# Pooled attention and two gated MLPs on one core: the order of work on every engine written out, piece by piece

## The chip, the cores and the metric

One Trainium2 chip, one of its cores. The metric is the device time of one execution, in microseconds (us). The kernel before takes 1108.62 us, the median of three runs (1107.89 to 1112.15). All weights and activations are computed on the core; nothing is prepared on the host except that float64 weights are passed as raw words.

## The reference, cut to what matters

```python
# q, k, v: [8 batches, 8 heads, 576, 64]
k_p = k.reshape(B, H, 72, 8, D).mean(axis=3)          # pooled keys and values
v_p = v.reshape(B, H, 72, 8, D).mean(axis=3)
scores = q @ k_p.T / sqrt(D)
attn = exp(scores - max(scores)); attn /= sum(attn) + 1e-9
x = concat_heads(attn @ v_p)                          # [8, 576, 512]
# first MLP
h = relu(x @ w_in)                                    # [8, 576, 1024]
conv = sum_k conv_w[k] * h[:, s + k - 1, :]           # 3 taps along the sequence, zero padded
x = (h * sigmoid(conv)) @ w_out                       # [8, 576, 512]
# second MLP
h = gelu_tanh(x @ w_in2)                              # [8, 576, 1024] -> u | v, 512 each
v = (v - mean(v)) / sqrt(var(v) + 1e-6) * g_ln
v = einsum('ts,bsd->btd', w_sg, v) + b_sg[:, None]    # along the sequence
out = x + (u * v) @ w_out2
```

## The kernel before, in words

Precision. Nearly every product is made of three TensorE matmuls on a high and a low part (`mm3`, L99 to L103, and the triples that `mm_sum`, L105 to L108, and `mm_halves`, L110 to L118, get). The high part is a ScalarE copy to the 32-bit matmul type, the low part a subtraction on VectorE or GpSimd (`subtract`, L141; `split`, L144). Weights come as float64 words and are put together on VectorE by three bit operations (`to_f32`, L172, L174, L176), then split.

Phase 1 is attention and the first MLP. Attention goes by batch, 8 batches: keys and values are pooled on GpSimd (`k_pool`, `v_pool`, L261 to L265), transposed on TensorE into `KBT` (`k_fin`, L285 to L288); queries are transposed in 32x32 blocks on VectorE (L340); then for each of five row tiles scores (`s_mm`, L361), maximum (L365), exponential (L376, or L370 with the sum accumulated in ScalarE), normalisation on GpSimd (`s_norm`, L387, L390), TensorE transposes (`e_tr`, L403, L409) and, for four head pairs, the product with the values (`a_mm`, L108 with tile `psa`, L435, L436). Its result goes into `xT`, which holds two batches. The MLP goes by 12 chunks of 384 rows, so three chunks are two batches; each chunk has eight slices f of the hidden width: `i_mm(c, f)` (L108 with tile `psi`, then L458, L468 on ScalarE, L469, L470 on VectorE, L471 on ScalarE, L474 on VectorE, a ScalarE copy and a GpSimd subtraction into `hg`) and `o_mm(c, f)` (L101 to L103 with tile `pso`). PSUM holds two banks for attention (tag `a`), three for `i_mm` (tag `i`) and three for `o_mm`.

Phase 2 is the second MLP by batch: `v_mm`, `u_mm`, `sp_mm`, `o2_mm`, on PSUM tiles `ps` of two banks. Its inputs are read back from DRAM (`x2s`), transposed on VectorE (`x2_fetch`, `x2_split`, L688) and split. Between the phases the spatial weights `w_sg` are transposed on TensorE (`sg_step`, L637, L640).

What sets the order. The function calls are written in program order (`phase1`, `att_steps`), but the tile framework is opened with a scheduler that runs a timeline model at build time and orders the instructions of each engine itself, one by one:

```python
with _tile.TileContext(nc, schedule_with_timeline_sim=True) as tc:
    pooled_attention_gated_mlps(tc, *args)
```

So in the trace matmuls of three `i_mm` calls and one `a_mm` call alternate singly. On the chip each engine then works through its own list in that order, and an instruction whose inputs are not there holds what stands behind it. All loads and stores are issued from SP's queue, in order too; pooled inputs go through two buffers (tag `raw`).

Of the kernel before, what the change touches and what calls it, by code (L numbers as in the profile page):

```python
# [38 lines left out]
):  # L39

# [27 lines left out]
    XW = 2 * (S + 2)  # L68

# [12 lines left out]
    def bank(tag, bufs):  # L82
        return psum1.tile([128, 512], F32, tag=tag, bufs=bufs, name=f"ps{tag}")

    def a_bank():
        return bank("a", 2)

    def i_bank():
        return bank("i", 3)
# [31 lines left out]

    ident = const.tile([128, 128], F32, name="ident")
# [20 lines left out]
    def split(hi, lo, x, eng=nc.vector):
        nc.scalar.copy(out=hi, in_=x)  # L144
        subtract(lo, x, hi, eng)


    def setup():
        nc.gpsimd.memset(mhalf, -0.5)
        nc.scalar.activation(out=warm, in_=mhalf, func=AF.Exp)  # L150
        make_identity(nc, ident)
        nc.vector.tensor_reduce(
            out=mask,
            in_=ident[0:96, 0:96].rearrange("p (k h j) -> p h k j", k=3, h=4),
            axis=AX.XY,
            op=ALU.add,
        )
        nc.gpsimd.memset(KBT, 0.0)
        for t in (Vh, Vl):
            nc.gpsimd.memset(t.bitcast(F32), 0.0)  # L160
# [17 lines left out]

    early = {}

    def load_coef():
        n = 3 * NF
        early["c"] = work.tile([128, 1, 512], F32, tag="y", name="cf")
        raw = early["cr"] = att2.tile([128, 1024], U32, tag="raw", name="craw")
        nc.sync.dma_start(out=raw[0:n, 0:256], in_=conv_w.rearrange("k (m p) -> (k m) p", p=256))
        nc.sync.dma_start(out=early["c"][n:n + NU, 0, 0:128], in_=g_ln.rearrange("(m p) -> m p", p=128))

    def setup_coef():
        n = 3 * NF
# [23 lines left out]
    def conv_weight(key, pool, tag, eng=None, bank_=None):  # L213
        raw = raws.pop(key)
        t = work.tile([128, 512], F32, tag="y", name="t")
        to_f32(raw, t, bank_)
        hl = pool.tile([128, 2, 512], F32R, tag=tag, name=f"{tag}hl")
        split(hl[:, 0, :], hl[:, 1, :], t, eng or nc.vector)
        return hl
# [15 lines left out]

    def load_pool(src, b, i, raw=None):


        if raw is None:
            raw = att2.tile([128, 2, 512], F32, tag="raw", name="raw")  # L240
# [15 lines left out]
        return raw  # L256

    def pool_sum(eng, raw, dst, n):
# [4 lines left out]
        eng.tensor_tensor(out=a[:, :, 0:256], in0=a[:, :, 0:256], in1=a[:, :, 256:512], op=ALU.add)  # L263
        eng.tensor_tensor(out=a[:, :, 0:128], in0=a[:, :, 0:128], in1=a[:, :, 128:256], op=ALU.add)
        eng.tensor_tensor(out=dst, in0=a[:, :, 0:64], in1=a[:, :, 64:128], op=ALU.add)  # L265
# [3 lines left out]
    def k_pool(b, i, eng, raw=None):  # L269
# [3 lines left out]
        if raw is None:  # L273
            raw = load_pool(k, b, i)
        if i < 2:
            pool_sum(eng, raw, kv["kp"][:, 2 * i:2 * i + 2, :], 128)
        else:
            pool_sum(eng, raw, kv["kr"], 32)

    def k_fin(b):  # L280
# [5 lines left out]
        nc.tensor.transpose(kt[:, :, 64:SP], kr.rearrange("p a d -> p (a d)"), ident[0:32, 0:32])  # L286
        nc.scalar.copy(out=KBT[0:64, :, 0:SP], in_=kt[0:64])
        nc.vector.tensor_copy(out=KBT[64:128, :, SP:2 * SP], in_=kt[64:128])  # L288

    def v_pool(b, i, eng, raw=None):  # L290
        if i == 0:
            kv["vp"] = att1.tile([128, NP_, D], F32, tag="vp", name="vp")
        if raw is None:
            raw = load_pool(v, b, i)
        if i < 2:
            pool_sum(eng, raw, kv["vp"][:, 2 * i:2 * i + 2, :], 128)
        else:
            kv["vr"] = att1.tile([96, 2, D], F32, tag="kr", name="vr")
            pool_sum(eng, raw, kv["vr"], 96)

    def v_fin(b, eng):
        vp = kv["vp"]
        for par in range(2):
            P = slice(64 * par, 64 * par + 64)
            split(Vh[P, :, 64 * par:64 * par + 64], Vl[P, :, 64 * par:64 * par + 64], vp[P])
        vrm = work.tile([96, NP_, 128], F32, tag="y", name="vrm")
        eng.tensor_tensor(
# [4 lines left out]
        )  # L312
        nc.scalar.copy(out=VR, in_=vrm)
        subtract(VR[32:64], vrm[32:64], VR[32:64])
# [5 lines left out]
    def q_load(b):  # L320
# [21 lines left out]

    def q_load0(t):
        t0, n = TT[t]
        nc.sync.dma_start(out=early["q"][0:n, t, :].rearrange("p (h d) -> p h d", h=H),
                          in_=q[0, :, t0:t0 + n, :].rearrange("h s d -> s h d"))

    es = {}

    def s_mm(b, t, act):  # L350


        n = TT[t][1]
        qT = qTs.pop((b, t))
        e = att2.tile([128, H, SP], F32, tag="e", name="e")
        sm = stat.tile([128, H], F32, tag="sm", name="sm")
        for a in range(2):
            ps = a_bank()
            for x in range(2):
                p = 2 * a + x  # L360
                nc.tensor.matmul(out=ps[0:n, 2 * SP * x:2 * SP * x + 2 * SP], lhsT=qT[:, p, 0:n], rhs=KBT[:, p, :],  # L361
                                 start=True, stop=True)
            sv = ps[0:n, 0:4 * SP].rearrange("p (x j) -> p x j", j=SP)
            mx = stat.tile([128, 4], F32, tag=f"mx{a}", name="mx")
            nc.vector.tensor_reduce(out=mx[0:n], in_=sv, axis=AX.X, op=ALU.max)  # L365
            if act:
                nc.vector.tensor_scalar(out=mx[0:n], in0=mx[0:n], scalar1=-EXP_SCALE, scalar2=None, op0=ALU.mult)
                for x in range(4):
# [3 lines left out]
            else:  # L372
                nc.vector.tensor_tensor(out=e[0:n, 4 * a:4 * a + 4, :], in0=sv, in1=bc(mx[0:n], 2, SP),  # L373
                                        op=ALU.subtract)
        if not act:
            nc.scalar.activation(out=e[0:n], in_=e[0:n], func=AF.Exp, scale=EXP_SCALE)  # L376
            nc.vector.tensor_reduce(out=sm[0:n], in_=e[0:n], axis=AX.X, op=ALU.add)
        es[b, t] = (e, sm)

    def s_norm(b, t, eng):  # L380
        n = TT[t][1]
        e, sm = es[b, t]
        rs = stat.tile([128, H], F32, tag="rs", name="rs")
        nc.vector.tensor_scalar(out=sm[0:n], in0=sm[0:n], scalar1=1e-9, scalar2=None, op0=ALU.add)
        nc.vector.reciprocal(out=rs[0:n], in_=sm[0:n])
        en = att2.tile([128, 512 + 192], F32, tag="en", name="en")
        eng.tensor_tensor(out=en[0:n, 0:512].rearrange("p (h j) -> p h j", h=H), in0=e[0:n, :, 0:64],  # L387
                          in1=bc(rs[0:n], 2, 64), op=ALU.mult)
        for c in range(2):
            eng.tensor_tensor(  # L390
# [5 lines left out]
    def e_tr(b, t):  # L396
# [5 lines left out]
        for c in range(NP_):  # L402
            nc.tensor.transpose(ps[:, 128 * c:128 * c + n], en[0:n, 128 * c:128 * c + 128], idn)  # L403
        m = ps.rearrange("p (c s) -> p c s", c=NP_)[:, :, 0:n]
        nc.scalar.copy(out=eTh[:, 0:NP_, T], in_=m)
        subtract(eTl[:, :, T], m, eTh[:, 0:NP_, T])
        ps = a_bank()
        for c in range(2):
            nc.tensor.transpose(ps[0:96, 128 * c:128 * c + n], en[0:n, 512 + 96 * c:608 + 96 * c], idn)  # L409
# [498 lines left out]
```

## Time and profile before

| | |
|---|---|
| median of three runs | 1108.62 us |
| the profiled execution's own time | 1111.01 us |
| its span, first to last instruction | 1109.2 us |
| TensorE busy | 996.8 us (90%) |
| VectorE busy | 670.4 us (60%) |
| ScalarE busy | 431.7 us (39%) |
| GpSimd busy | 316.5 us (29%) |
| mean granted TensorE clock | 0.957 of full speed |
| moved by DMA | 86.65 MB, mean 78 GB/s |

The profile is one execution. "Busy" of TensorE counts a matmul from its start to its modelled end, and neighbours overlap, so what a matmul costs in a dense stretch is read from the distance of starts, not from its duration. The granted clock has two levels, 1.00 (2.4 GHz) and 0.50 (1.2 GHz); a mean between them says for how much of a stretch the lower one held.

### The profile page before, as it was taken

The numbers are of one execution on the slowest core, as the hardware profiler recorded it, in microseconds if no ns is written. First come the engines' busy times: TensorE is split into PE (matmuls) and PEld (weight loads), VectorE is DVE, ScalarE is ACT, GpSimd is POOL, SyncE is SP. The second block draws the span as 40 slices with busy tenths as digits, with TensorE's granted clock in tenths as the row PEclk, the third lists the DMA queues.
The fourth block names the chain that finished last, engine by engine and source line by source line (L and its number), as shares of the span: only waits on it lengthen the run. The fifth ranks groups of instructions, "written<-read, shape, count | busy, mean of one in ns | idle before, by whom it ended". The sixth has DMA issues, their size and how long they took to land.

```text
span 1109.2 us, 14835 instructions
## 1 busy us (share of the span) xinstructions
PE 996.8 (90%) x5446; PEld 890.8 (80%) x5446; DVE 670.4 (60%) x1258; ACT 431.7 (39%) x892; POOL 316.5 (29%) x418
## 2 busy tenths in 40 slices
PE   3467789999799988999897996999999999999997
PEld 2356679889689877898887885989898989999896
DVE  4949967648387376684665946764634545373523
ACT  2444446535266354555554643422222222231210
POOL 3357646426267155462240320100100010000000
PEclk9998989999689999899998997999999999999999
DMA  9944227014133134130004039241414231322021
GB/s 220 259 113 90 54 63 104 29 53 99 45 65 74 48 71 105 44 77 29 29 29 158 6 76 233 33 102 33 110 29 111 42 108 32 87 33 95 1 76 57
DMA packets 182836, 86.65 MB, mean 78 GB/s; under 512 B 150800, under 2 KB 154924, under 8 KB 182764
## 3 DMA queue, kind: packets, MB, share of 16 engines
q1 hardware_dynamic: 182764, 85.71, 30.9%
q8 instruction: 43, 0.70, 0.3%
q14 instruction: 29, 0.24, 0.1%
HBM read 66.81 MB, written 18.87 MB: 77 GB/s over the span
## 4 chain that ended last, share of the span: by engine, by line
PE 71%; DVE 9%; DMA 6%; SPq 5%; POOL 3%; ACT 3%; issue 2%; DVEq 0%; POOLq 0%; ACTq 0%
PE ps L114 20%; PE psi L108 13%; PE ps L101 6%; PE ps L103 6%; PE ps L102 6%; PE pso L103 4%; PE pso L102 4%; PE pso L101 4%; PE psa L108 3%; DMA raw<-in_k_dram 2%; SPq L324 2%; PE psa L361 2%; DMA raw<-in_v_dram 2%; DVE psi L470 1%; POOL raw L263 1%
## 5 line engine op out<-in xcount | busy, mean ns | idle before, releaser
L141 POOL TENSOR_TENSOR hg<-g,hg 128x384 fp32r<-128x384 f32 x96 | 99.9, 1042 | 112.7 <-ACT hg L144 112.6
L759 POOL TENSOR_SCALAR rstd<-mv 128x2 f32<-128x2 f32 (+1 forms) x20 | 8.0, 398 | 371.4 <-DVE mv L757 371.4
L800 DVE SCALAR_TENSOR_TENSOR y<-ps,coef,bsg 128x576 f32<-128x576 f32 x32 | 26.2, 818 | 125.6 <-PE ps L114 125.6
L114 PE MATMUL ps<-w2sh,v 128*128 128x288 f32 x512 | 94.5, 296 | 0.0
L361 PE MATMUL psa<-KBT,qT 128*128 128x144 f32 (+1 forms) x320 | 60.9, 332 | 28.3 <-DVE e L373 17.7
L361 PEld LDWEIGHTS psa<-KBT,qT 128*128 128x128 f32 (+1 forms) x320 | 51.8, 209 | 36.7 <-issue 20.7
L114 PEld LDWEIGHTS ps<-w2sh,v 128*128 128x128 f32 x512 | 76.9, 189 | 0.0
L263 POOL TENSOR_TENSOR raw<-raw 128x512 f32<-128x512 f32 (+2 forms) x42 | 53.8, 1288 | 75.4 <-DMA raw<-in_v_dram 41.0
L436 DVE SCALAR_TENSOR_TENSOR xl<-psa,xh 128x288 fp32r<-128x288 f32 x64 | 29.3, 458 | 75.8 <-ACT xh L435 74.9
L469 DVE SCALAR_TENSOR_TENSOR psi<-h,coef,psi 128x384 f32<-128x384 f32 x96 | 58.7, 612 | 18.6 <-ACT psi L468 18.0
L144 ACT CAST hg<-g 128x384 fp32r<-128x384 f32 x96 | 49.1, 512 | 48.4 <-DVE g L474 47.5
L787 ACT ACTIVATE u<-ps 128x576 f32<-128x576 f32 x32 | 20.9, 652 | 115.9 <-PE ps L114 115.9
L471 ACT ACTIVATE psi<-psi 128x384 f32<-128x384 f32 x96 | 45.3, 472 | 52.0 <-DVE psi L470 51.8
L470 DVE SCALAR_TENSOR_TENSOR psi<-h,coef,psi 128x384 f32<-128x384 f32 x96 | 58.7, 614 | 1.0
L474 DVE SCALAR_TENSOR_TENSOR g<-psi,h 128x384 f32<-128x384 f32 x96 | 52.4, 546 | 10.0 <-ACT psi L471 9.3
L458 ACT ACTIVATE h<-psi 128x386 f32<-128x386 f32 (+1 forms) x96 | 46.3, 491 | 27.3 <-PE psi L108 27.2
L468 ACT ACTIVATE psi<-h,coef 128x384 f32<-128x384 f32 x96 | 55.6, 583 | 2.0
L144 ACT CAST gt<-y 128x576 fp32r<-128x576 f32 (+2 forms) x48 | 23.1, 512 | 85.1 <-DVE y L802 85.1
L114 PE MATMUL ps<-w2sl,v 128*128 128x288 f32 x256 | 54.9, 295 | 0.0
L435 ACT ACTIVATE xh<-psa 128x288 fp32r<-128x288 f32 x64 | 26.4, 412 | 72.4 <-PE psa L108 70.9
L387 POOL TENSOR_TENSOR en<-e,rs 128x512 f32<-128x512 f32 (+1 forms) x40 | 42.5, 1064 | 38.8 <-PE psa L409 16.2
L365 DVE TENSOR_REDUCE mx<-psa 128x4 f32<-128x288 f32 (+1 forms) x80 | 35.6, 450 | 25.3 <-PE psa L361 24.6
(414 smaller groups left out, 3011.0 us busy)
## 6 DMA issues: line engine op xcount, KB each, us to landing
xb<-x2s SPq DMA_DIRECT2D x128, 72.0 KB
x2s<-ob SPq DMA_DIRECT2D x32, 256.0 KB
res<-x2s SPq DMA_DIRECT2D x16, 512.0 KB
out_dram<-ob SPq DMA_DIRECT2D x16, 512.0 KB
qb<-in_q_dram SPq DMA_DIRECT2D x112, 72.0 KB
raw<-in_k_dram SPq DMA_DIRECT2D x28, 256.0 KB
raw<-in_v_dram SPq DMA_DIRECT2D x28, 256.0 KB
raw<-in_v_dram SPq DMA_DIRECT2D x48, 64.0 KB
```

The source lines that it names most:

```text
L101: nc.tensor.matmul(out=out_, lhsT=ah, rhs=bh, start=first, stop=False)
L102: nc.tensor.matmul(out=out_, lhsT=al, rhs=bh, start=False, stop=False)
L103: nc.tensor.matmul(out=out_, lhsT=ah, rhs=bl, start=False, stop=last)
L108: nc.tensor.matmul(out=out_, lhsT=a, rhs=b_, start=(i == 0), stop=(i == n - 1))
L114: nc.tensor.matmul(out=ps[:, hf, 0:HS], lhsT=a, rhs=b_[:, hf * HS:(hf + 1) * HS], start=(i == 0), stop=(i == n - 1),)
L141: eng.tensor_tensor(out=out, in0=in0, in1=hi.bitcast(F32), op=ALU.subtract)
L144: nc.scalar.copy(out=hi, in_=x)
L263: eng.tensor_tensor(out=a[:, :, 0:256], in0=a[:, :, 0:256], in1=a[:, :, 256:512], op=ALU.add)
L361: nc.tensor.matmul(out=ps[0:n, 2 * SP * x:2 * SP * x + 2 * SP], lhsT=qT[:, p, 0:n], rhs=KBT[:, p, :], start=True, stop=True)
L468: nc.scalar.activation(out=y, in_=tap(1), func=AF.Copy, scale=cw(1, f))
L469: nc.vector.scalar_tensor_tensor(out=y, in0=tap(0), scalar=cw(0, f), in1=y, op0=ALU.mult, op1=ALU.add)
L470: nc.vector.scalar_tensor_tensor(out=y, in0=tap(2), scalar=cw(2, f), in1=y, op0=ALU.mult, op1=ALU.add)
```

## The change: what it does

Every function becomes a generator (a *task*) that yields wherever the work passes from one engine to another; the stretch between two yields is a *piece*, and all of its instructions are on one engine. A string `ORDER` names tasks by letter, slice and batch or chunk (`I6.4` is slice 6 of `i_mm` in chunk 4; `s0.5` is score tile 0 of batch 5); each time a name comes up, its next piece is issued. `step` adds to each instruction an ordering edge without a semaphore to the one before it on the same engine, so the scheduler can no longer move it. SP's queue is ordered the same way.

Beside that:

- PSUM: attention has three banks, `i_mm` two (before two and three).
- The low parts of all 16 weight slices of the first MLP are subtracted on GpSimd (before: 8 on VectorE, 8 on GpSimd), and `to_f32` keeps its intermediate in the output tile in SBUF (before: in a PSUM bank of tag `i`).
- Score tiles 0, 2 and 4 of batch 1 too take the exponential with the sum accumulated on ScalarE (before: those of batch 0 alone).
- Of the keys of batch b+1 one half is loaded and pooled ahead of the score tiles of batch b, the rest between and behind the last of them; the values of batch b are pooled ahead of its score tiles.
- `w_sg` is loaded into buffers of tag `ob` and transposed among the pieces of chunks 10 and 11 (before: in the steps around and behind the last `o_mm` calls).
- Phase 2 has the same calls in the same TensorE order.

```diff
+ORDER = '''z k0.0 k1.0 k2.0 p0.0 c z z p1.0 v0.0 p2.0 v1.0 p3.0 v2.0 p4.0 i0 i1 z z i2 ... i7 q.1 t0 ... t7 k0.0
...
+ e0.5 I4.5 e0.5 O5.4 O5.4 p3.5 e0.5 I4.5 s1.5 e0.5 s2.5 s1.5 I4.5 I5.5 s2.5 I4.5 I4.5 s2.5 I5.5 e1.5 s2.5 O6.4
+ O6.4 I4.5 I5.5 s2.5 I4.5 e1.5 s2.5 I6.5 I5.5 I5.5 s2.5 e1.5 I5.5 p4.5 e1.5 s3.5 I6.5 q.6 O7.4 I5.5 s3.5 e1.5
...
+ o0.7 o1.7 o0.7 m2.7 m2.7 o0.7 o2.7 o1.7 o1.7 o2.7 o2.7'''
...
+    ACT_SUM = {(0,0),(0,2),(0,4),(1,0),(1,2),(1,4)}
...
     def a_bank():
-        return bank("a", 2)
+        return psum1.tile([128, 512], F32, tag="a", bufs=3, name="psa")
     def i_bank():
-        return bank("i", 3)
+        return psum1.tile([128, 512], F32, tag="i", bufs=2, name="psi")
...
+    LO_IN = [pool for f in range(NF)]
+    LO_OUT = [pool for f in range(NF)]
...
+    def weight(pool_, tag, src, eng, bank_, done):
+        raw = pool_.tile([128, 1024], U32, tag=tag, name=f"{tag}raw")
...
+        nc.sync.dma_start(out=dst, in_=src)
+        yield
         t = work.tile([128, 512], F32, tag="y", name="t")
-        to_f32(raw, t, bank_)
...
+        yield from to_f32(raw, t, bank_() if bank_ else None)
+        hl = pool_.tile([128, 2, 512], F32R, tag=tag, name=f"{tag}hl")
+        done(hl)
+        nc.scalar.copy(out=hl[:, 0, :], in_=t)
+        yield
+        subtract(hl[:, 1, :], t, hl[:, 0, :], eng)
...
+    def t_w_in(f, *_):
...
+        return weight(in1, f"wi{f}", src, LO_IN[f], None, done)
...
-    def i_mm(c, f):
+    def t_i(f, c):
...
         mm_sum(ps[:, 0:w], prs)
+        yield
...
         nc.scalar.activation(out=y, in_=tap(1), func=AF.Copy, scale=cw(1, f))
+        yield
         nc.vector.scalar_tensor_tensor(out=y, in0=tap(0), scalar=cw(0, f), in1=y, op0=ALU.mult, op1=ALU.add)
         nc.vector.scalar_tensor_tensor(out=y, in0=tap(2), scalar=cw(2, f), in1=y, op0=ALU.mult, op1=ALU.add)
+        yield
         nc.scalar.activation(out=y, in_=y, func=AF.Tanh, scale=0.5)
+        yield
...
+        yield
+        nc.scalar.copy(out=hg[:, 0, f, :], in_=g)
+        yield
+        subtract(hg[:, 1, f, :], g, hg[:, 0, f, :], pool)
...
+    def t_sg(i, *_):
         t0, n = TT[i]
-        wn = wns[i] = x2["3"].tile([128, S + REM], F32, tag="vg", name="wn")
+        wn = outp.tile([128, 2, 512], F32, tag="ob", name="wn").rearrange("p a s -> p (a s)")
...
+    pin = mybir.DependencyInfo(mybir.DependencyClass.NoSync, mybir.DependencyReason.DATA)
+    def step(key):
+        if key not in running:
+            i, _, b = key[1:].partition(".")
+            running[key] = iter(tasks[key[0]](int(i or 0), int(b or 0)) or ())
+        more = next(running[key], 0)
+        issued = nc.cur_bb.bb.instructions
+        for n in range(seen[0], len(issued)):
+            ins = issued[n]
+            if ins.engine in last:
+                tc.add_manual_dep(ins, last[ins.engine], pin, reason="order")
+            last[ins.engine] = ins.name
+        seen[0] = len(issued)
+        return more is None
+    for key in ORDER.split():
+        step(key)
```

Letters: `i`, `t`, `w`, `l` the weights w_in, w_out, w_in2, w_out2; `k`, `K`, `v`, `V` keys and values; `q` the query load of a batch, `p` a query tile's transpose; `s`, `e`, `a` scores, transposes and the product with the values; `I`, `O` `i_mm` and `o_mm`; `g` the tiles of w_sg; `y`, `r` the inputs of phase 2; `n`, `u`, `d`, `o` its four products; `m` the residual load; `A`, `B`, `C` the hand-over of memory.

Read for TensorE alone, the stretch of `ORDER` from the second half of s1.4 to e2.4 is: s1.4, O0.3, e0.4, O1.3, e0.4, s2.4, I1.4, s2.4, e1.4, O2.3, I2.4, e1.4, s3.4, O3.3, s3.4, e2.4. The same alternation holds for batches 3 to 7. GpSimd's list from the keys of batch 5 on is: k1.5 three times, s0.4, I6.3, I7.3, s1.4, I0.4, s2.4, I1.4, I2.4, s3.4, V.4, I3.4, k0.5 three times, s4.4. On VectorE the first query transpose of a batch (p0) stands behind the last one of the batch before (p4) by five or six `I` and `O` pieces of TensorE, and `q`, the load between them, is issued right behind p4. In the first batches TensorE's list is: all of batch 0 up to a3.0, I0.0, I1.0, the score tiles and transposes of batch 1 up to e3.1, I2.0, I3.0, e3.1, e4.1, a0.1, O0.0, I4.0 and so on, with s0.2 to s3.2 and I0.1 to I3.1 before O7.0.

## Rows read from the trace of the kernel before

**Rows 1.** Windows by stage: length, busy us (instructions) of each engine, clock, DMA.
```profile
0.00:143.30 143.30, 83.05 (x374) 66.73 (x375) 105.61 (x199) 56.96 (x150) 76.43 (x105) 0.95 0.58 146
...
290.40:437.40 147.00, 136.49 (x712) 121.96 (x710) 95.11 (x200) 73.13 (x156) 72.23 (x93) 0.93 0.28 67
...
584.40:678.67 94.27, 79.65 (x394) 70.31 (x393) 62.70 (x110) 47.20 (x100) 18.48 (x16) 0.92 0.34 102
678.67:1109.20 430.53, 423.81 (x2544) 386.87 (x2544) 214.88 (x356) 108.01 (x177) 22.77 (x40) 0.99 0.28 69
```

**Rows 2.** Waits of TensorE over the whole span: total us, times, longest.
```profile
PE psa L361 <- DVE e L373: 17.7, 9, 6.8
...
PE psa L637 <- DVE w2sl L141: 8.1, 4, 3.2
```

**Rows 3.** Windows inside one period: a stretch at half clock, a dense one.
```profile
282.50:299.50 17.00, 13.05 (x46) 10.89 (x47) 6.01 (x13) 5.33 (x12) 3.63 (x7) 0.50 0.13 47
...
336.00:392.00 56.00, 56.00 (x307) 50.27 (x306) 30.31 (x62) 26.62 (x59) 19.61 (x25) 1.00 0.20 57
```

**Rows 4.** Timeline of TensorE, 290 to 345: start, duration, instruction.
```profile
333.61 0.40 PE L101 MATMUL pso<-w3hl,hg 128*128 128x512 f32 x1
...
335.67 0.34 PE L108 MATMUL psi<-xh,wi0hl 128*128 128x386 f32 x1
...
336.73 1.14 PE L361 MATMUL psa<-KBT,qT 128*128 128x144 f32 x8
337.62 0.43 PE L108 MATMUL psi<-xh,wi0hl 128*128 128x386 f32 x1
...
338.77 0.34 PE L108 MATMUL psi<-xh,wi1hl 128*128 128x386 f32 x1
...
340.88 0.34 PE L108 MATMUL psi<-xh,wi2hl 128*128 128x386 f32 x1
```

**Rows 5.** Timeline of VectorE, 336.5 to 345: the reciprocal of that score tile.
```profile
342.76 0.20 DVE L385 RECIPROCAL rs<-sm 128x8 f32<-128x8 f32 x1
```

**Rows 6.** Timeline of GpSimd, 336.5 to 350.
```profile
344.40 1.30 POOL L263 TENSOR_TENSOR raw<-raw 96x512 f32<-96x512 f32 x1 [1.13 <-DMA raw<-in_v_dram]
...
346.48 1.04 POOL L387 TENSOR_TENSOR en<-e,rs 128x512 f32<-128x512 f32 x1
```

**Rows 7.** Chain that ended last, window 600 to 700: start, us, what.
```profile
639.76 0.40 ACT h L458
...
643.30 0.51 ACT hg L144
...
655.92 0.57 DVE g L474
...
678.67 0.80 PE ps L101
```

**Rows 8.** Timeline of SP's queue, 0 to 150.
```profile
47.78 4.30 SPq L245 DMA_DIRECT2D raw<-in_k_dram  x4
```

**Rows 9.** Timeline of GpSimd, 0 to 170: the keys' last piece of batch 1.
```profile
68.94 1.28 POOL L263 TENSOR_TENSOR raw<-raw 32x512 f32<-32x512 f32 x1 [3.21 <-DMA raw<-in_k_dram]
```

**Rows 10.** Timeline of SP's queue, 140 to 690: one batch's queries.
```profile
327.28 8.46 SPq L324 DMA_DIRECT2D qb<-in_q_dram  x16
```

**Rows 11.** VectorE's groups, 590 to 640: busy us, mean ns.
```profile
L141 DVE TENSOR_TENSOR w211hl<-t,w211hl 128x512 fp32r<-128x512 f32 x1 | 1.5, 1503 | 0.0
...
L174 DVE SCALAR_TENSOR_TENSOR t<-w201raw,t 128x512 uint32<-128x512 uint32 x1 | 1.0, 1037 | 0.0
...
L174 DVE SCALAR_TENSOR_TENSOR t<-w211raw,t 128x512 uint32<-128x512 uint32 x1 | 0.7, 679 | 0.0
```

**Rows 12.** ScalarE's groups, 0 to 143.3.
```profile
L370 ACT ACTIVATE e<-psa,mx 128x72 f32<-128x72 f32 x16 | 4.9, 324 | 2.8 <-DVE mx L367 2.8
...
L376 ACT ACTIVATE e<-e 128x576 f32<-128x576 f32 x6 | 4.1, 681 | 5.5 <-DVE e L373 5.5
...
L370 ACT ACTIVATION_READ_ACCUMULATOR e<-psa,mx 128x1 f32 x16 | 3.3, 209 | 0.0
```

More of the change, by code (lines that the diff above doesn't have):

```diff
@@ L138, in pooled_attention_gated_mlps @@
     eTl = att1.tile([128, NP_, S], F32R, name="eTl")
+    hg = slot.tile([128, 2, NF, CH], F32R, tag="hg", name="hg")
     def subtract(out, in0, hi, eng=nc.vector):
         eng.tensor_tensor(out=out, in0=in0, in1=hi.bitcast(F32), op=ALU.subtract)
[L143 to L160, printed above, removed]
     def to_f32(raw, t, tmp=None):
@@ L286, in k_fin, with t_v, t_vfin @@
         nc.tensor.transpose(kt[:, :, 64:SP], kr.rearrange("p a d -> p (a d)"), ident[0:32, 0:32])
+        yield
         nc.scalar.copy(out=KBT[0:64, :, 0:SP], in_=kt[0:64])
+        yield
         nc.vector.tensor_copy(out=KBT[64:128, :, SP:2 * SP], in_=kt[64:128])
-    def v_pool(b, i, eng, raw=None):
+    def t_v(i, b):
+        raw = raw_tile(v, b, i)
+        load_pool(v, b, i, raw)
+        yield
+        eng = dve if b == 0 and i else pool
         if i == 0:
             kv["vp"] = att1.tile([128, NP_, D], F32, tag="vp", name="vp")
-        if raw is None:
-            raw = load_pool(v, b, i)
         if i < 2:
-            pool_sum(eng, raw, kv["vp"][:, 2 * i:2 * i + 2, :], 128)
+            yield from pool_sum(eng, raw, kv["vp"][:, 2 * i:2 * i + 2, :], 128)
         else:
             kv["vr"] = att1.tile([96, 2, D], F32, tag="kr", name="vr")
-            pool_sum(eng, raw, kv["vr"], 96)
-    def v_fin(b, eng):
+            yield from pool_sum(eng, raw, kv["vr"], 96)
+    def t_vfin(_, b):
         vp = kv["vp"]
-        for par in range(2):
-            P = slice(64 * par, 64 * par + 64)
-            split(Vh[P, :, 64 * par:64 * par + 64], Vl[P, :, 64 * par:64 * par + 64], vp[P])
+        quads = [slice(64 * par, 64 * par + 64) for par in range(2)]
+        for P in quads:
+            nc.scalar.copy(out=Vh[P, :, P], in_=vp[P])
+        yield
+        for P in quads:
+            subtract(Vl[P, :, P], vp[P], Vh[P, :, P])
+        yield
         vrm = work.tile([96, NP_, 128], F32, tag="y", name="vrm")
-        eng.tensor_tensor(
+        pool.tensor_tensor(
             out=vrm.rearrange("p (c a) (x d) -> p c (a x) d", c=2, x=2),
@@ L613, in w2_open @@
         nc.sync.dma_start(out=w2["b"], in_=bc(b_sg, 0, 128))
-        pieces = [(kt, e) for e in (1, 0) for kt in range(KC)]
-        for kt, e in pieces:
-            load_w((kt, e), p, f"w2{kt}{e}", w_in2[kt * 128:(kt + 1) * 128, 1024 * e:1024 * e + 1024])
-        def step(kt, e):
-            w2[kt, e] = conv_weight((kt, e), p, f"w2{kt}{e}")
-        return [lambda kt=kt, e=e: step(kt, e) for kt, e in pieces]
-    wns = {}
-    def sg_load(i):
+        for t in ("sh", "sl"):
+            w2[t] = p.tile([128, NM + 1, S], F32R, tag=t, name=f"w2{t}")
@@ L645, in pooled_attention_gated_mlps, with t_x2_open @@
     x2 = {}
-    def x2_open():
-        for t in ("sh", "sl"):
-            w2[t] = w2["p"].tile([128, NM + 1, S], F32R, tag=t, name=f"w2{t}")
+    def t_x2_open(*_):
+        in1_ctx.close()
         p = ctx.enter_context(tc.tile_pool(name="x21", bufs=1))
@@ L682, in x2_fetch, with t_x2_rest @@
                 in_=x2s[b][:, c0:c0 + 32].rearrange("(g i) d -> i g d", i=32))
-        xbs[b, kt] = xb
-    def x2_split(b, kt):
-        xb = xbs.pop((b, kt))
+        yield
         xt = work.tile([128, S], F32, tag="y", name="xt")
         nc.vector.transpose(out=xt, in_=xb)
-        split(x2[b % 2][0][:, kt, :], x2[b % 2][1][:, kt, :], xt)
-    def x2_rest_fetch(b):
+        yield
+        xh, xl = (a[:, kt, :] for a in x2[b % 2])
+        nc.scalar.copy(out=xh, in_=xt)
+        yield
+        subtract(xl, xt, xh)
+    def t_x2_rest(_, b):
         xb = x2["2"].tile([128, DM], F32, tag="xb", name="xbr")
@@ L726, in rows @@
         return [(buf[REM * e:REM * e + REM, 0, :], dst[b - 1 + e][128 * NM:S, :]) for e in range(2)]
-    def o_tiles(b):
-        n = NM + (b % 2)
-        return [list(range(i, min(i + 2, n))) for i in range(0, n, 2)]
     def segs(b):
@@ L736, in segs, with tiles_of, t_v2 @@
         return [(0, m, 0), (m, REM, m + REM)]
-    vgs = {}
-    def v_mm(b, tiles):
+    def tiles_of(i):
+        return list(range(2 * i, min(2 * i + 2, NM + 1)))
+    def t_v2(i, b):
+        tiles = tiles_of(i)
+        nt = len(tiles)
         ps = ps_tile()
@@ L760, in v_mm @@
         nc.gpsimd.tensor_tensor(out=rs[:, 0:nt], in0=rs[:, 0:nt], in1=mhalf[:, 0:nt], op=ALU.pow)
[L761 to L764 removed]
+        yield
         for j, i in enumerate(tiles):
@@ L767, in v_norm @@
                                     op0=ALU.subtract, op1=ALU.mult)
-            if i < NM:
-                split(g2["v", i][:, 0, :], g2["v", i][:, 1, :], vg[:, j, :])
-        if tiles[0] == NM:
+        yield
+        if tiles[0] < NM:
+            for j, i in enumerate(tiles):
+                nc.scalar.copy(out=g2["v", i][:, 0, :], in_=vg[:, j, :])
+            yield
+            for j, i in enumerate(tiles):
+                subtract(g2["v", i][:, 1, :], vg[:, j, :], g2["v", i][:, 0, :])
+        else:
             x = vg[:, 0, :]
@@ L802, in sp_mm, with t_res @@
         nc.vector.tensor_tensor(out=y, in0=y, in1=g2["u"][:, d, :], op=ALU.mult)
+        yield
         for s0, n, o in segs(b):
-            split(g2["gh"][:, d, o:o + n], g2["gl"][:, d, o:o + n], y[:, s0:s0 + n])
+            nc.scalar.copy(out=g2["gh"][:, d, o:o + n], in_=y[:, s0:s0 + n])
+        yield
+        for s0, n, o in segs(b):
+            subtract(g2["gl"][:, d, o:o + n], y[:, s0:s0 + n], g2["gh"][:, d, o:o + n])
     ress = {}
-    def res_load(b, tiles):
+    def t_res(i, b):
+        tiles = tiles_of(i)
         res = x2["3"].tile([128, 2, 512], F32, tag="res", name="res")
```

429 lines of the change are left out of this document (166 added, 263 removed).

## The prediction

> **What bounds the kernel now.** I read the windows by stage first [rows 1]: five stages, of which the second to fourth are alike (147.1, 147.0 and 147.0 us; one is shown). Each of these three periods is three chunks and two batches of attention. The reader is to see that TensorE is the busiest engine from 143 us on, with 136.5 of 147.0 us in a period and 423.8 of 430.5 in phase 2, and that it leads neither in the start-up (83 of 143, VectorE 106) nor fully in the hand-over (79.7 of 94.3). Then the waits of TensorE [rows 2]: no single long one; the largest are short waits for a score tile's subtraction (nine, 17.7 us in all) and, in the hand-over, four for the `w_sg` tiles (8.1 us). Third, windows inside a period [rows 3]: in 282.5 to 299.5 the granted clock is 0.50, the lower level (1.2 GHz); in 336 to 392 it is 1.00 and TensorE is busy 56.0 of 56.0. Ahead of the slow stretch TensorE had stood idle. So a short wait costs twice: once as idle time, and again as matmuls at half clock.
>
> **What a period costs when TensorE never waits.** From the distance of starts [rows 4]: one `O` piece is nine matmuls from 333.61 to 335.67, 2.06 us; one `I` piece twelve from 338.77 to 340.88, 2.11 us; a score tile takes 0.89 us for eight recorded matmuls, 0.11 each. A period has 24 of each of the first two, 24 x 4.17 = 100.1 us, and 712 - 504 = 208 recorded matmuls of attention [rows 1], 22.9 us at 0.11: at least 123. From above: 307 matmuls take 56.00 us in the dense window [rows 3], so 712 take 129.9. I take 128, nearer the second, since its mix is the same. Of 147.0 us 19 are then lost: 10.5 idle, the rest half clock (in the 17 us window alone, 13.05 busy at 0.50 is 6.5).
>
> **The order in the periods.** `ORDER` puts an `O` or `I` piece between almost any two attention pieces that depend on each other. Two distances decide.
>
> First, the PSUM banks of `I`, now two. From the first ScalarE instruction of a slice to its last reader of the bank takes 639.76 to 643.3, 3.5 us [rows 7]. Between the end of one `I` and the start of the next but one stand O, I, O: 6.2 us. Slack 2.7 us; the lost bank costs nothing while VectorE is not that far behind. Between two users of an attention bank (three now) there are likewise 3 us or more.
>
> Second, the score tiles. In the tile shown there [rows 4] the scores start at 336.73 and the normalisation ends at 347.5 [rows 6], 10.8 us. `ORDER` has O, O, I and some 1.4 us of small pieces between s1.4 and e1.4, 7.6 us. It would be late by 3 us were the delay the same. But the reciprocal was done at 342.96 [rows 5], and GpSimd began at 346.48, since ahead of it in its list stood a pooling step whose values came by DMA at 344.4 [rows 6]: 3.5 us. In the new list no pooling that waits for a load stands between s0 and s3. Without it 7.3 us: the tile fits by 0.3. So I don't put the waits at zero: 0.3 us for ten tiles, 3 us a period. A period is 131 us (bounds 125 and 147), 16 less; three of them, 48 us.
>
> The same 96 slices, 8 batches and DMAs are issued as before. Of the moved loads, q's sixteen DMAs hold SP's queue for 8.46 us [rows 10], and stand ahead of keys and stores there as before; they are a rival below.
>
> **The start-up, to 143.3 us.** VectorE is busy 105.6 us of it, 74% [rows 1]. The loads limit it first: batch 1's keys are issued at 47.78 behind all weights [rows 8], and their last piece is summed from 68.94 on, after a wait for DMA [rows 9]. `ORDER` keeps keys behind weights on SP, so batch 1's scores start at about 71 as now. What changes is what stands ahead of O7.0: also a.1, I0.1 to I3.1 and some four score tiles of batch 2, which before come after 143.3: 4.3 + 8.4 + 4.5, 17 us of TensorE (estimated at the prices above). VectorE loses eight subtractions of 0.68 us (the shape's undisturbed time) [rows 11], 5.4 us, and gets about an eighth of a period's 95 us more, 12: 112 us. At the same 75% busy O7.0 comes at 150; at 81% at 138, at 70% at 160. The single edits lie in these bounds: GpSimd (76 of 143 busy) gets eight subtractions of about 1.3 us; the sum on ScalarE makes a tile there 8 x (0.324 + 0.209) = 4.3 us instead of 0.68 [rows 12], 3.6 more for three tiles, hidden on an engine busy 57 of 143, or up to 10.8 where the tiles chain; the scratch in SBUF costs a bit operation between nothing and 0.36 us (679 and 1037 ns) [rows 11]. I take 150: 7 us later than 143.3 with 17 more done, about 10 gained; I count 8, since the two-bank rotation starts there.
>
> The Trainium skill (SBUF — State Buffer, Who interferes with whom) says that a VectorE instruction with two SBUF inputs and a GpSimd instruction that reads SBUF shut each other out for a whole instruction. The 1037 and 1503 ns [rows 11] against 679 agree. It speaks against this change, where 32 bit operations get a second SBUF input while GpSimd gets more work.
>
> **The hand-over, 584.4 to 678.7.** 16 slices are 66.7 us, 58 other matmuls 6.4: 73 of 94.3. The four waits for `w_sg` go (8.1 us with what they hold), since its tiles now stand between `O` and `I` pieces with time to spare. What is late next: from the last slice's final VectorE step (655.92) to phase 2's first matmul (678.67) pass 22.7 us [rows 7], in which `x2s` is read back, transposed and split. Behind I7.11 `ORDER` has 8 `O` pieces, 16.5 us, and some 3 us of transposes, so a few us of idle remain. I take 80 us (bounds 76 and 92): 14 gained.
>
> **Phase 2** has the same TensorE order and is full; its first matmuls come out of less idle: 2 gained (bounds 4 gained, 3 lost).
>
> **Sum.** 48 + 8 + 14 + 2 = 72. The profiled execution took 1111.0 (span 1109.2, 1.8 around it): 1039. The median of the runs is 2.4 below it: **1037 us**. Its own range: 1008 (periods of 125, O7.0 at 140, all bounds low) to 1056 (periods of 136).
>
> **Rivals.**
> - *Half the gain.* Lists kept in order on four engines: whatever is late holds everything behind it. For it: the score tile fits by 0.3 us, and half clock follows short waits. Against it: VectorE has 95 of 131 us, GpSimd 72. Periods of 139: 24 lost, start-up 3 more: 1064. Chance 0.20.
> - *The start-up chokes on the shared access.* 32 bit operations at 0.36 us more are 11.5, with GpSimd's delay O7.0 at 166: 1053. For it: [rows 11]. Against it: such operations also fall into gaps. Chance 0.12. This is what the skill's rule would make of it; [rows 11] alone give the price.
> - *The waits only move.* The new order's waits on p, e or banks take the place of the old, periods stay 147, start-up as long: only the hand-over gains 5, 1104. Against it: in [rows 3] the engines keep up with a full TensorE for 56 us. Chance 0.05.
> - *Slower: the queries.* Place: p0 of the next batch in VectorE's list, behind p4 by 10.4 to 12.5 us of `I` and `O` and 2 to 2.5 of small pieces, 12.4 to 15 us. The load takes 8.46 us to issue [rows 10] and about 3.2 to land (the wait in [rows 9]), 11.7: it fits by 0.7. If SP reaches it late, VectorE stands at p0, and slices and scores behind it. Price: late by 10, TensorE loses 10 less the slack of 2.7, and 6.5 at half clock behind it: 14 for each of six batches, 84: 1121. It decides from 9 us of lateness on. For it: one in-order queue. Against it: DMA is busy 0.28 in a period [rows 1]. Chance 0.08.
>
> That the order isn't changed at all is no rival: singly alternating matmuls can't come from whole pieces.
>
> **How the numbers follow.** Forecast 0.55, rivals 0.20, 0.12, 0.05, 0.08. Range 1008 to 1082: it holds the forecast and the first two rivals with room for both together (1080); out are the last two and a tail at each end. A measurement tells some 0.5%, 5.5 us, from no change. Faster 0.87 (the first three cases), same 0.05 (the fourth), slower 0.08.
>
> **What would show it.** Periods of 128 to 134 us with a clock of 0.98 or more; O7.0 at 140 to 160; TensorE waiting under 4 us a period; no wait of VectorE for `qb`; `w_sg` transposes without a wait; a gap under 6 us ahead of phase 2. Wrong if the clock in the periods stays at 0.93, or VectorE or GpSimd is full in them, or if the start-up runs past 166.

## The result, and the profile after

The changed kernel takes 1057.8 us (median of four runs, 1054.0 to 1060.3) against 1110.1 for the kernel before (four runs, 1107.9 to 1112.2): ratio 0.953, interval 0.949 to 0.956. Forecast were 1037 us and a range of 1008 to 1082; the forecast without its rivals ended at 1056. The profiled execution took 1058.6 us, span 1056.8: 52.4 us less than before, where the working says 72.

First the windows, cut at the same times in both kernels (columns as in [rows 1]); the kernel before:

```profile
0.00:180.00 180.00, 117.19 (x557) 98.74 (x558) 132.33 (x257) 77.03 (x193) 94.07 (x129) 0.94 0.54 131
180.00:600.00 420.00, 389.19 (x2022) 347.55 (x2020) 266.00 (x548) 205.03 (x436) 181.23 (x235) 0.93 0.24 57
```

And the changed kernel, whose phase 2 begins at 627.72:

```profile
0.00:180.00 180.00, 120.81 (x549) 102.23 (x550) 144.88 (x266) 83.35 (x243) 111.21 (x141) 0.79 0.59 129
180.00:600.00 420.00, 418.66 (x2278) 375.44 (x2278) 309.89 (x608) 241.00 (x503) 198.69 (x245) 1.00 0.26 70
600.00:627.72 27.72, 17.40 (x82) 13.26 (x81) 14.89 (x27) 8.04 (x17) 1.17 (x2) 0.89 1.02 242
627.72:1056.80 429.08, 423.95 (x2540) 386.21 (x2540) 214.36 (x348) 106.93 (x175) 19.76 (x40) 0.99 0.26 63
```

Count the matmuls: at 180 us both kernels have done about as many (557 and 549). In the next 420 us TensorE does 2278 instead of 2022, idle for 1.3 us instead of 30.8 and at clock 1.00 instead of 0.93: 256 matmuls at 420/2278 = 0.184 us are 47 us, nearly the whole gain. Phase 2 lasts 429.1 us (430.5 in [rows 1]).

The periods, by TensorE's timeline at the first matmul of the second, fifth and eighth chunk's last `O` piece:

```profile
222.79 0.49 PE L107 MATMUL pso<-w7hl,hg 128*128 128x512 f32 x1
...
351.74 0.49 PE L107 MATMUL pso<-w7hl,hg 128*128 128x512 f32 x1
...
480.69 0.49 PE L107 MATMUL pso<-w7hl,hg 128*128 128x512 f32 x1
```

They lie 128.95 us apart, where [rows 1] has 147.0. TensorE's waits from 180 to 600 us (total, times, longest) are nine lines in the kernel before, of which this is the largest, and a single one in the changed kernel, below it:

```profile
PE psa L361 <- DVE e L373: 8.0, 6, 1.4
```
```profile
PE psi L114 <- DVE g L521: 1.3, 2, 0.7
```

The hand-over in TensorE's timeline: the last transposes of phase 1, those of the rest rows, phase 2's first matmul.

```profile
617.68 0.27 PE L581 MATMUL psa<-ident,wn 64*128 64x64 f32 x1
625.23 1.08 PE L627 MATMUL psa<-ident,xbr 128*128 128x128 f32 x4 [7.28 <-DMA w7raw<-in_moe_w_out_dram]
627.72 0.80 PE L107 MATMUL ps<-w201hl,x2h 128*128 128x512 f32 x1 [1.40 <-DVE x2rl L151]
```

The reader is to see 8.7 us of waiting where the forecast had a few. The name behind the arrow is that of a transfer on the same queue; what the transposes read is `xbr`, whose load SP issues late:

```profile
616.68 1.60 SPq L220 DMA_DIRECT2D w5raw<-in_moe_w_out_dram  x1
618.38 0.38 SPq L220 DMA_DIRECT2D w6raw<-in_moe_w_out_dram  x1
618.85 1.09 SPq L623 DMA_DIRECT2D xbr<-x2s  x2
```

The issue ends at 619.94, and 5.3 us more pass until the transposes. The DMA share of the stretch from 600 us on is 1.02, so the transfers under way may hold the load up as much as the late issue; the two are not told apart here.

### The profile page after: what moved, and what is told of

The parts are those of the page before. It is cut to its first block, busy times and chain, and to the rows that moved or that the text cites. A ratio compares the mean times of both kernels' runs of the same rounds, so it can differ in the third digit from the quotient of the medians.

```text
span 1056.8 us, 14906 instructions
## 1 busy us (share of the span) xinstructions
PE 980.8 (93%) x5446; PEld 877.1 (83%) x5446; DVE 684.0 (65%) x1247; ACT 439.3 (42%) x937; POOL 330.8 (31%) x426
## 4 chain that ended last, share of the span: by engine, by line
PE 78%; DVE 10%; SPq 4%; DMA 4%; ACT 1%; issue 1%; POOL 1%; DVEq 0%; POOLq 0%; ACTq 0%
PE ps L120 21%; PE psi L114 16%; PE ps L107 6%; PE ps L108 6%; PE ps L109 6%; PE pso L107 5%; PE pso L109 5%; PE pso L108 5%; PE psa L396 3%; PE psa L114 3%; SPq L220 1%; SPq L355 1%; PE psa L441 1%; DMA raw<-in_k_dram 1%; DVE t L169 1%
## 5 line engine op out<-in xcount | busy, mean ns | idle before, releaser
L692 POOL TENSOR_SCALAR rstd<-mv 128x2 f32<-128x2 f32 (+1 forms) x20 | 5.3, 264 | 377.2 <-DVE mv L689 376.9
L770 DVE TENSOR_TENSOR ob<-ps,res 128x1024 f32<-128x1024 f32 (+1 forms) x20 | 22.3, 1117 | 32.5 <-PE ps L109 32.4
L120 PEld LDWEIGHTS ps<-w2sl,v 128*128 128x128 f32 x256 | 41.1, 188 | 0.0
```

Source lines behind the costliest of these rows:

```text
L120: nc.tensor.matmul(out=ps[:, hf, 0:HS], lhsT=a, rhs=b_[:, hf * HS:(hf + 1) * HS], start=(i == 0), stop=(i == n - 1),)
```

## The experiments

Marks used below: "O7.0" is the start of the first chunk's last `O` piece, 162.2 us in the changed kernel; "idle" is TensorE's idle time from 180 to 600 us.

**The kept order and the PSUM banks, each alone and neither.** e1_free:

```diff
-            if ins.engine in last:
-                tc.add_manual_dep(ins, last[ins.engine], pin, reason="order")
```

> The changed kernel with its pieces written in the same order, but nothing that keeps that order on the engines: the scheduler places the instructions again. Theory (the kept order carries the gain): TensorE is again held up several times in each period, the periods (128.5 to 128.9 us in the changed kernel) go back to 141 to 150 us, and the time is 1095 to 1115 us. Rival (the other edits carry it: third score bank, exponentials summed on ScalarE, low halves on GpSimd, loads half a batch ahead): periods stay under 132 us and the time is 1052 to 1066 us.

e2_banks (order kept), and e6_free_banks (both edits):

```diff
-        return psum1.tile([128, 512], F32, tag="a", bufs=3, name="psa")
+        return psum1.tile([128, 512], F32, tag="a", bufs=2, name="psa")
...
-        return psum1.tile([128, 512], F32, tag="i", bufs=2, name="psi")
+        return psum1.tile([128, 512], F32, tag="i", bufs=3, name="psi")
```

> The changed kernel with the PSUM banks as they were before it: two for the short tiles (psa), three for the first MLP's input tiles (psi); the order is kept as it is. Theory (the order is the gain and the bank moved gives little): periods 128 to 132 us, time 1056 to 1066 us. Rival (the third short bank is what lets TensorE go on without waiting): a score tile's second half, its 0.89 us, waits for the eviction of the first at most of the 5 x 4 halves of a batch, about 1 us each, so periods of 140 us and more and a time over 1085 us.

> Order not kept, as in e1_free, and also the PSUM banks as before (two psa, three psi). TensorE's idle time between 180 and 600 us was 30.8 us in the kernel before, 12.4 in e1_free, 1.3 in the changed kernel. Theory (the third psa bank is what gave e1_free most of its gain, since the scheduler no longer stalls on evictions of short tiles): idle time there over 22 us, time 1098 to 1112 us. Rival (the gain of e1_free comes from the list of single pieces and from the loads ahead; the bank is worth what it was in e2_banks, 10 us, most of it ahead of 180 us): idle time 10 to 18 us, time 1086 to 1097 us.

Measured:

| | three `psa` banks | two `psa` banks |
|---|---|---|
| order kept | 1057.8, ratio 0.953 (0.949 to 0.956) | e2: 1069.0, 0.964 (0.959 to 0.968) |
| order free | e1: 1085.2, 0.978 (0.972 to 0.983) | e6: 1130.7, 1.018 (1.011 to 1.024) |

The same stretch, 180 to 600 us, of e1_free, e2_banks and e6_free_banks:

```profile
180.00:600.00 420.00, 407.60 (x2213) 362.38 (x2212) 295.07 (x589) 224.89 (x482) 189.38 (x238) 1.00 0.26 67
```
```profile
180.00:600.00 420.00, 415.21 (x2259) 372.30 (x2259) 309.60 (x610) 238.38 (x499) 200.75 (x250) 1.00 0.27 71
```
```profile
180.00:600.00 420.00, 380.09 (x1990) 336.08 (x1989) 264.12 (x543) 200.13 (x430) 181.48 (x235) 0.94 0.25 58
```

TensorE's largest wait in that stretch of e6_free_banks is the one for the normalised scores:

```profile
PE psa L441 <- POOL en L425: 26.8, 4, 9.1
```

e1_free missed both expectations: 27 us slower without the kept order, not 37 to 57 (the theory) and not under 9 (the rival); its two periods by the same marks are 128.5 and 136.8 us. Its idle is 12.4 us; much of the rest comes behind 600 us, where its last `O` piece begins 13 us later and its phase 2 at 653.3 us, 26 later. e2_banks is 3 us above the theory's range; its periods (129.4 us) are as the theory has them, and most of its loss is there by 230 us (O7.1 at 230.5 instead of 222.8). e6_free_banks is 19 us above the theory's range and slower than the kernel before. Its idle is 39.9 us, over 22 as the theory has it, but the largest wait, the line above, is not for a bank, as the theory has it: it is for normalised scores. How the missing bank leads to it is not shown. So the gains of the two edits overlap: the third bank (taken from `i_mm`) is worth 45 us to a free order and 11 to the kept one; keeping the order is worth 27 us with three banks and 62 with two. Without both, what is left of the change loses 20 us (1.8%).

**Keys fetched late.** e7_keys_late, for each of k0, k1, k2 from batch 2 on:

```diff
-... k0.3 (SP: load) ... [half a batch] ... k0.3 (GpSimd: first sum) ...
+... [half a batch] ... k0.3 (SP: load) k0.3 (GpSimd: first sum) ...
```

> The changed kernel, order kept, but from batch 2 on each of the three key loads is issued on SP directly ahead of the first of its sums on GpSimd instead of half a batch ahead. Theory (the early load is needed, since GpSimd's list is kept in order): GpSimd stands at each of 18 first sums for 2 to 4 us until the load lands, the low halves and normalised scores behind it come late, TensorE is idle 10 us or more between 180 and 600 us, and the time is 1068 to 1090 us. Rival (the sums themselves are half a batch early and GpSimd is busy only half of the time, so nothing on TensorE's path waits): idle time under 5 us, time 1055 to 1062 us.

1068.1 us, ratio 0.962 (0.957 to 0.967), idle from 180 to 600 us 4.2 us: the theory's time and the rival's idle. Two waits make most of it, those of GpSimd that end at 102 and 179 us. GpSimd, then TensorE:

```profile
102.05 1.26 POOL L280 TENSOR_TENSOR raw<-raw 128x512 f32<-128x512 f32 x1 [9.27 <-DMA raw<-in_k_dram]
...
178.74 1.26 POOL L280 TENSOR_TENSOR raw<-raw 128x512 f32<-128x512 f32 x1 [8.37 <-DMA raw<-in_k_dram]
179.96 1.04 POOL L425 TENSOR_TENSOR en<-e,rs 128x512 f32<-128x512 f32 x1
```
```profile
104.37 1.12 PE L441 MATMUL psa<-ident,en 128*128 128x128 f32 x4 [7.88 <-POOL en L425]
...
181.05 1.11 PE L441 MATMUL psa<-ident,en 128*128 128x128 f32 x4 [7.00 <-POOL en L425]
```

Both loads stand on SP right behind a batch's sixteen query loads:

```profile
87.80 8.47 SPq L355 DMA_DIRECT2D qb<-in_q_dram  x16
96.37 3.38 SPq L252 DMA_DIRECT2D raw<-in_k_dram  x4
...
164.72 8.43 SPq L355 DMA_DIRECT2D qb<-in_q_dram  x16
173.25 0.44 SPq L552 DMA_DIRECT2D x2s<-ob  x1
173.79 1.27 SPq L252 DMA_DIRECT2D raw<-in_k_dram  x2
```

O7.0 comes 2.6 us later than in the changed kernel, O7.1 7.0 and phase 2 7.8. GpSimd's list alone puts the scores' normalisation behind the sum (its reciprocal was done at 171.9, and GpSimd had been idle since 170.4): that is what a kept list costs when a load is late. At the later first sums GpSimd waits 1.2 to 4.6 us, but there is slack: the periods stay at 129 us.

**The start-up.** e3_lo and e5_early:

```diff
-    LO_IN = [pool for f in range(NF)]
-    LO_OUT = [pool for f in range(NF)]
+    LO_IN = [(dve, pool)[f % 2] for f in range(NF)]
+    LO_OUT = [(dve, pool)[f % 2] for f in range(NF)]
```
```diff
-    LO_OUT = [pool for f in range(NF)]
+    LO_OUT = [dve if f < 3 else pool for f in range(NF)]
...
-... I0.0 (ScalarE) ... I1.0 (ScalarE) ... K.1 ... t0 ... t1 ... t2 ...
+... t0 I0.0 (ScalarE) ... I1.0 (ScalarE) t1 t2 ... K.1 ...
```

> The changed kernel with the low halves of the first MLP's sixteen weights alternating between VectorE and GpSimd, as before the change, instead of all on GpSimd. Theory (VectorE's whole work binds the start-up): eight subtractions of 0.68 us come back to VectorE, 5.4 us, and about half of the 14.6 us go that its bit operations take beyond their undisturbed 0.42 and 0.68 us; the two nearly cancel, O7.0 begins at 159 to 163 us and the time is 1054 to 1060 us. Rival (the shared access is what chokes the start-up): the bit operations return to within 4 us of their undisturbed time, O7.0 at 153 to 157 us, time 1048 to 1053 us.

> The changed kernel with the first three first-MLP output weights (t0 to t2) converted in the time in which VectorE stands idle for batch 1's keys (62 to 74 us), their low halves on VectorE instead of GpSimd. Theory (the start-up is bound by VectorE, 93% busy from 84 to 168 us): three times the 1.8 to 5.7 us that these conversions take there leave that stretch, O7.0 begins at 153 to 157 us instead of 162.2, and the time is 1048 to 1053 us. Rival 1 (the stretch is bound by TensorE's order and its half clock): O7.0 at 160 to 163 us, time 1055 to 1060 us. Rival 2 (GpSimd's key sums from 64 to 73.5 us slow down beside VectorE's conversions): batch 1's last key transposition moves from 73.6 us to 76 us or later, and O7.0 comes no earlier than 160 us.

e3_lo: O7.0 at 160.2, 1056.9 us, ratio 0.952 (0.947 to 0.957), no difference, as the theory has it; of the 14.6 us a quarter went, not half (the bit operations take 39.6 us instead of 43.1). GpSimd has 10 us less to do up to O7.0 there, and O7.0 hardly moves. e5_early: O7.0 at 157.1, the theory's edge, and 1055.8 us, 0.951 (0.947 to 0.955), the first rival's time. In e8_both, with the same start-up, O7.0 is at 160.8; so an effect of 2 to 4 us is not told from one profile, and e5_early stays open.

e9_one_bit_op, e11_no_low (both on the first MLP's output weights) and e10_act_sum:

```diff
-        nc.vector.scalar_tensor_tensor(out=mi, in0=up, scalar=0xC0000000, ...)
-        nc.vector.scalar_tensor_tensor(out=ti, in0=lo, scalar=29, ...)
```
```diff
-        subtract(hl[:, 1, :], t, hl[:, 0, :], eng)
+        pool.memset(hl[:, 1, :].bitcast(F32), 0.0)
```
```diff
-    ACT_SUM = {(0,0),(0,2),(0,4),(1,0),(1,2),(1,4)}
+    ACT_SUM = {(0,0),(0,2),(0,4)}
```

> The changed kernel without the second and third of the three bit operations on each of the eight first-MLP output weights (those weights are then not the right numbers): sixteen VectorE operations of 0.68 us undisturbed less ahead of O7.0, 10.9 us. Everything else, the order too, is as it was. Theory (VectorE's work binds the start-up): O7.0 begins at 149 to 155 us (162.2 in the changed kernel) and the time is 1045 to 1052 us. Rival (GpSimd's work, or the chain of scores with its half clock, binds it): O7.0 at 158 us or later, time 1054 to 1060 us.

> The changed kernel with the low halves of the eight first-MLP output weights set to zero by a GpSimd memset of about 0.5 us instead of GpSimd's subtraction of about 1.28 us (so those weights keep only their high halves): GpSimd has about 6 us less ahead of O7.0 and reads no SBUF for them; VectorE's list is the same. Theory (VectorE binds): O7.0 moves only by what the bit operations' 14.6 us of excess lose, a part of it: 157 to 161 us, time 1052 to 1058 us. Rival (GpSimd binds the start-up): O7.0 at 150 to 156 us, time 1045 to 1051 us.

> The changed kernel with the exponentials of batch 1's tiles 0, 2 and 4 done as before the change: the maximum subtracted on VectorE, one exponential of the tile on ScalarE, the sum on VectorE. VectorE gets three times about 1.4 us more, ScalarE loses three times about 3.6 us. Theory (VectorE binds the start-up): O7.0 1 to 4 us later, time 1058 to 1063 us. Rival (the tile's eight short exponentials in a row on ScalarE are what the scores wait for): O7.0 at 153 to 159 us, time 1049 to 1055 us.

| | O7.0 | VectorE, GpSimd, ScalarE busy up to it | us, ratio |
|---|---|---|---|
| changed kernel | 162.2 | 128.5, 99.8, 72.0 | 1057.8, 0.953 |
| e9_one_bit_op | 153.4 | 113.0, 95.6, 71.9 | 1048.8, 0.944 (0.940 to 0.947) |
| e11_no_low | 156.7 | 125.3, 93.8, 73.1 | 1054.7, 0.950 (0.948 to 0.952) |
| e10_act_sum | 157.9 | 128.5, 100.0, 66.6 | 1054.7, 0.950 (0.947 to 0.952) |

e9 does what the theory says: 15.5 us less on VectorE, O7.0 8.8 us earlier. e11's time lies in the theory's range, its O7.0 0.3 us ahead of it. e10 goes against the theory and lies in the rival's ranges, for O7.0 and for the time: VectorE's load is the same, and O7.0 is no later. Whether it is really earlier stays open (its interval overlaps the changed kernel's), but summing on ScalarE for batch 1 brings nothing. So VectorE's work holds much of the start-up; that it holds all of it is not shown. The granted clock up to O7.0 does not order these runs: 0.78 in the changed kernel, 0.83 in e9, 0.76 in e11, 0.81 in e10, and 0.87 in e2_banks, whose O7.0 is the latest of these at 168.1.

**The hand-over.** e4_hand, and e8_both, which adds e5_early's start-up:

```diff
-... y2.0 l0 y3.0 l1 l2 r.0 l3 ...                       (SP: loads)
+... y2.0 y3.0 r.0 l0 l1 l2 l3 ...                       (e4_hand, e8_both)
-... r.0 n0.0 n1.0 n2.0 ...                              (TensorE)
+... n0.0 r.0 n1.0 n2.0 ...                              (e4_hand, e8_both)
-... l0 l1 l2 l3 n0.0 r.0 ...                            (ScalarE, e4_hand)
+... l0 r.0 n0.0 l1 l2 l3 ...                            (ScalarE, e8_both)
```

> The changed kernel with the hand-over reordered: the last column block of batch 0 (y3.0) and the rest rows (r.0) are loaded ahead of the second MLP's output weights, the split of y3.0 on ScalarE and VectorE comes directly behind its transposition, and the rest rows' transpositions on TensorE stand behind the first phase-2 tile instead of ahead of it. Theory (the 10 us between O7.11's end at 617.8 and phase 2's first matmul at 627.72 are the wait for the rest rows, queued on SP behind output weights): the first matmul comes at 622 to 624 us, when y3.0's low half is there, and the time falls by 4 to 6 us, to 1052 to 1054 us. Rival (the load of y3.0 and the half clock hold phase 2 anyway, or the output weights then come late for the first output tile): first matmul at 626 us or later, time 1056 to 1060 us.

> The start-up of e5_early and a second try at the hand-over: as in e4_hand, but the eviction and split of the rest rows stand ahead of the last three output weights' conversions on ScalarE and VectorE, and ahead of the first tile's GELU on ScalarE, instead of behind them. Theory (in e4_hand the 7 us gained ahead of phase 2 were lost again because TensorE, behind n1.0, waited 7.1 us for the rest rows' two halves): phase 2 begins at 615 to 617 us and lasts 429 to 431 us, time 1045 to 1049 us. Rival (phase 2's early tiles are held by something else, the half clock after the gap or the output weights): phase 2 lasts 435 us or more again, time 1052 us or more.

e4_hand starts phase 2 at 620.6 us, 7.2 earlier and ahead of the theory's range, and gains nothing: 1060.6 us, 0.955 (0.951 to 0.959), 0.6 us above the rival's range. The rest rows' load is issued at 618.15, only 0.7 us earlier than in the changed kernel, although it stands ahead of the output weights; what phase 2 no longer waits for are its transposes. TensorE's timeline in e4_hand shows the rest rows' transposes at once, and their product twice waited for:

```profile
620.56 0.47 PE L107 MATMUL ps<-w201hl,x2h 128*128 128x512 f32 x1 [2.38 <-ACT ob L546]
627.75 0.60 PE L627 MATMUL ps<-ident,xbr 128*128 128x128 f32 x4
637.45 0.51 PE L107 MATMUL ps<-w201hl,x2rh 128*128 128x512 f32 x1 [3.52 <-ACT x2rh L630]
641.60 0.80 PE L108 MATMUL ps<-w201hl,x2rl 128*128 128x512 f32 x1 [3.64 <-DVE x2rl L151]
```

In e8_both these waits are gone: the first matmul comes at 617.85 and phase 2 lasts 431.6 us instead of 439.2:

```profile
617.85 0.74 PE L107 MATMUL ps<-w201hl,x2h 128*128 128x512 f32 x1 [2.36 <-ACT ob L546]
625.07 0.60 PE L627 MATMUL ps<-ident,xbr 128*128 128x128 f32 x4
```

1048.5 us, ratio 0.945 (0.940 to 0.950): the theory, at its upper edge (start and length of phase 2 each lie under 1 us above its bounds).

e12_best is e8_both with `LO_IN` as in e3_lo:

> The kernel of e8_both (1048.5 us) with the low halves of the first MLP's input weights alternating between VectorE and GpSimd as in e3_lo. Theory (that split is neutral, as e3_lo showed): 1045 to 1051 us. Rival (the two gains of the start-up add up): O7.0 at 154 to 157 us, 1042 to 1045 us.

1049.6 us, 0.946 (0.943 to 0.949), O7.0 at 159.4, phase 2 from 617.6: no difference to e8_both. These two are the fastest here that leave none of the work out, about 61 us below the kernel before and 8 to 9 below the changed kernel; the intervals of their ratios end where the changed kernel's begins (0.950 and 0.949 against 0.949).

## Why the prediction was right or wrong

*The number: inside the range by the room for rivals.* 1057.8 lies 2 us above the end of the forecast without its rivals, 1056. (That range is not added up rightly: 18, 10, 4 and 2 us below 1037 are 1003, not 1008, and periods of 136 alone give 1052.) The rival of half the gain is near in its number, 1064, and not in its mechanism, periods of 139; the rival of the shared access came true in the main, as told below.

*The periods: right.* Forecast 131 us each and 48 gained; measured 128.95. Only two whole periods stand so in the changed kernel (from O7.7 to O7.10 it is 112.3 us, since attention comes to its end); three of them would be 54 gained, and counted by matmuls the 420 us gave 47. The dense price of 128 holds to 1 us. The 3 us added for a score tile that "fits by 0.3 us" were not there: no wait for it in 180 to 600 us.

*Why they are full: half the reason.* The prediction gave the whole to the order and priced the bank of `I` that was lost, rightly at little in the periods (1.3 us of waiting; ahead of 180 us it is 7.5). It never priced the third bank of the short tiles. The table of four shows it to be worth 45 us where the scheduler places the instructions.

*The start-up: the step that failed.* "At the same 75% busy O7.0 comes at 150": it came at 162.2, above the bound of 160. The busy share was 79%, within the assumed 70 to 81%; the work was mis-sized, 128.5 us of VectorE instead of 112. And 162.2 is 18.9 us later than 143.3 with 107 more matmuls done (481 against 374), 19.7 us at 0.184: of the 8 us gained there is about nothing, and at 180 us 549 matmuls stand against 557.

Most of the 16.5 us too little lies in the bit operations, whose scratch is now in SBUF; the prediction priced that at up to 0.36 us an operation and left it out of the 112. The 48 bit operations took 32.7 us in the kernel before, each 0.67 to 0.70; in the changed kernel they take 43.1, 10.4 more, and 14.6 over what they take undisturbed (16 at 0.42, 32 at 0.68). The rest is the work moved ahead of O7.0, about 19 us of VectorE instead of the 12 estimated. The 15 bit operations that took over 0.15 us longer than undisturbed all ran beside a GpSimd instruction; of the other 33, 16 ran beside none. So this is in the main the rival of the shared access, which had 11.5 us and O7.0 at 166. It counted only the 32 operations with two inputs, though: 8.2 of the 14.6 us are on the 16 with one. No run puts the scratch alone back into PSUM: the 10.4 us are read from two traces. One operation in the kernel before, and the same one, the worst, in the changed kernel, both in VectorE's timeline, then GpSimd's beside the latter:

```profile
90.97 0.68 DVE L172 TENSOR_SCALAR psi<-w2raw 128x512 uint32<-128x512 uint32 x1
```
```profile
113.89 3.60 DVE L163 TENSOR_SCALAR t<-w2raw 128x512 uint32<-128x512 uint32 x1
```
```profile
113.28 1.28 POOL L282 TENSOR_TENSOR raw<-raw 32x256 f32<-32x256 f32 x1
114.54 1.01 POOL L151 TENSOR_TENSOR hg<-g,hg 128x384 fp32r<-128x384 f32 x1
115.52 0.45 POOL L284 TENSOR_TENSOR kr<-raw 32x128 f32<-32x128 f32 x1
115.93 1.27 POOL L151 TENSOR_TENSOR w1hl<-t,w1hl 128x512 fp32r<-128x512 f32 x1
```

It ends 0.3 us after the fourth of GpSimd's instructions in a row. The Trainium skill (SBUF — State Buffer, Who interferes with whom) lets the later one wait until the other's instruction has finished; in the trace it is not done until behind four.

*The hand-over: mis-sized, 14 forecast.* Booked with three periods, 54, and 1.4 from phase 2, the span's 52.4 leave start-up and hand-over together 3 us longer than before; booked by matmuls (1.5 us lost by 180 us, 47 gained up to 600, 1.4 in phase 2), about 5 us are gained behind 600 us. Either way it is not the 22 forecast for the two. The `w_sg` waits went, as forecast (1.6 us left). What was late next was named, the read-back, but put at "a few us": it was 8.7, since the rest rows' transposes stand ahead of phase 2 in TensorE's list and their load comes late, issued at 618.85 behind output weights, at a DMA share of 1.02. e8_both gets 9.9 us less ahead of phase 2 than the changed kernel, part of it from the start-up (2.7 us at O7.1, 220.1 instead of 222.8).

*Slower by the queries: did not happen.* No wait of VectorE for `qb` in the periods. The mechanism behind it, a load held on the one queue behind sixteen query loads and a list kept in order that turns it into TensorE's idle time, is real, though: e7_keys_late shows it with the keys, at 7.9 and 7.0 us of TensorE's waiting. In the changed kernel the keys are loaded half a batch ahead.

## What to carry to other kernels

A kept order and one more PSUM bank can gain the same time; measure the four combinations before giving one of them the gain. Count a start-up by its binding engine's work, each operation at the price it has beside the other engines, not undisturbed. When a wait ahead of a stage is taken away, follow the delayed tile to its next consumer: e4_hand gained 7 us and lost them again in the next 21.

## What was not expected of the hardware

A VectorE operation of 0.42 us took 3.60 us beside back-to-back GpSimd instructions. And one start-up order, run twice, put the same matmul at 157.1 and at 160.8 us (e5_early, e8_both), another at 162.2 and 161.9 (the changed kernel, e4_hand), while the periods behind it repeat to 0.1 us.
